# Other partition layout for the q and k tiles, logits as plain float32 products, and 64 transfers for v in an attention and mixture-of-experts kernel

## The chip, the cores and the metric

The kernel runs on one core of a Trainium2 chip. The metric is the time of one execution on the device in microseconds (us); the median of the runs shown is compared. The engines of the core work side by side: PE multiplies matrices (PEld is its loading of weights), DVE, ACT and POOL (GpSimd) work element by element, and SP issues most of the transfers (DMA).

## The reference

What must be computed, cut to what matters here: attention inside chunks of 64 tokens, a routed mixture of 8 experts, and a dense layer with three inputs to a maximum.

```python
B, H, S, D = 8, 8, 576, 64                      # q, k, v: (B, H, S, D), float32
scores = (1 / sqrt(D)) * q_c @ k_c.T            # in each chunk of 64 tokens
attn = softmax(scores); x = attn @ v_c          # x: (B*S = 4608, H*D = 512)
skip = x @ w_skip; compute = skip > 0           # w_skip: (512,)
logits = x[compute] @ w_gate                    # w_gate: (512, 8)
e = argmax(logits); g = softmax(logits)[e]
x[compute] += g * (relu(x[compute] @ w1[e]) @ w2[e])
h = max(x @ m2_w1, x @ m2_w2, x @ m2_w3); out = h @ m2_w_out
```

## The kernel before, in words

The program has three stages. The first, which the change touches, does attention and routing; the second runs the experts on gathered rows; the third is the dense layer.

**Units and steps.** The 4608 tokens are cut into 18 units of 256 tokens (q and k of a unit are loaded together) and 36 tiles of 128 tokens. One loop runs over `t`, 36 tiles and a lag, and everything of a step is written there; a unit `u` is two steps. PE's order is the written order. The order of the other engines comes from a scheduler.

**Loads.** `load_qk(u)` (L212) puts q and k of a unit into tiles of 128 partitions. A partition holds two tokens of all eight heads, so a packet is 512 bytes, and a unit that lies in one batch entry takes one transfer of 128 partitions for q and one for k. A unit across a boundary of batch entries (576 tokens each) takes two for each, with fewer partitions. `load_v(u)` (L221) loads v chunk by chunk of 64 tokens, even heads into partitions 0 to 63 and odd heads into 64 to 127: 64 KB and 64 partitions each, 144 transfers in all. Loads run five units ahead for q and k and three for v. SP takes its transfers in order, and one that must wait for a buffer holds those behind it.

**Turning.** `pair_heads` (L230) copies each half of q and k into an order in which two heads lie side by side: q by POOL, k (`kr`) by DVE. Three buffers each of `qr` and `kr`. `qk_transpose` (L245) turns them on PE, four 128x128 transposes for each of q and k in a step, and ACT copies the result out (L247).

**A step on PE** is, in this order: `values` of tile t-2 (L290, `xp`), `scores` of tile t (L260, `sc`), the transposes of tile t-1's exponentials (L277, `trp`), in every second step the logits (L333, `lt`), the transposes of q and k for unit u+1 (`trq`, `trk`), the transposes of tile t-2's rows (L318, `trx`), and in every other second step the logits' way back (L341, `lp`). DVE makes the maximum and the difference (L264, L266) and the scaled rows (L303 to L305).

**Logits.** The turned rows are split into a rounded part `xh` (ACT, L325) and the remainder `xl` (DVE, L326). Eight products of 18 rows by 256 tokens with the split gate weights `wr` give the logits turned (`lt`), ACT copies them (L335), and two float32 products with a small matrix `fold` bring them back to one token a partition (`lp`). The gates `wcat` are loaded behind unit 4 (L590, L591) and split by ACT and DVE (L592, L593).

**Routing.** For each group of four tiles, `route` does some twenty small DVE operations, `place` two small products (`rk`, L409, L410) and the slots, `store_x` sends 1040 KB of rows to memory on POOL's queue (L470), and `send_id` scatters ids in four indirect transfers by POOL (L448). Weights of expert 0 are loaded and split in the last third of the stage (L91).

Of the kernel before, what the change touches and what calls it, by code (L numbers as in the profile page):

```python
# [37 lines left out]
def kernel(  # L38
# [45 lines left out]
    def ps_sm(name):  # L84
        return ps("sm", name)
# [54 lines left out]
    wr = kpool.tile([P, KC, 2 * R], F32R, name="wr")  # L140
    fold = kpool.tile([P, R], F32, name="fold")
    lgT = kpool.tile([P, UT], F32, name="lgT")
    nc.gpsimd.memset(lgT, 0.0)
    nc.gpsimd.memset(fold, 0.0)
    for base in (0, -R):
        nc.gpsimd.affine_select(
            out=fold, in_=fold, compare_op=ALU.not_equal, fill=1.0, base=base,
            pattern=[[-1, R]], channel_multiplier=1,
        )
# [33 lines left out]
    NV = 4  # L183
    v_all = [apool.tile([P, 4, 4, D + 1], F32, name=f"v_all{i}", bufs=1) for i in range(NV)]
# [16 lines left out]
    def load_qk(u):  # L201
        if u % 5 < 3:
            qt = four_kb([P, H, 2 * D], F32, f"qt{u}", u % 5 == 2)
            kt = four_kb([P, H, 2 * D], F32, f"kt{u}", u % 5 == 2)
        else:
            both = bpool.tile([P, 2, H, 2 * D], F32, tag="b8", name=f"qkt{u}")
            qt, kt = both[:, 0], both[:, 1]
        for h0, h1 in [(0, 4), (4, 8)] if u == 0 else [(0, 8)]:
            for off, b, s, n in pieces(u):
                pr = slice(off // 2, (off + n) // 2)  # L210
                for dst, src in ((qt, q), (kt, k)):
                    link["load"] = nc.sync.dma_start(  # L212
                        dst[pr, h0:h1], src[b, h0:h1, s:s + n, :].rearrange("h (p r) d -> p h (r d)", r=2))
        units[u] = {"qt": qt, "kt": kt}

    def load_v(u):
        vb = v_all[u % NV]
        for off, b, s, n in pieces(u):
            for c in range(n // 64):
                for par in range(2):  # L220
                    link["load"] = nc.sync.dma_start(  # L221
                        vb[64 * par:64 * par + 64, off // 64 + c, :, :D],
                        v[b, par::2, s + 64 * c:s + 64 * c + 64, :].rearrange("hp k d -> k hp d"),
                    )
# [923 lines left out]
```

## Time and profile before

| | |
|---|---|
| median of 3 runs | 1119.62 us (1119.02 to 1122.96) |
| the profiled execution's own time | 1127.18 us |
| its span, first to last instruction | 1125.4 us |
| PE busy | 1024.9 us, 91% of the span |
| DVE, ACT, POOL busy | 596.0, 420.8, 326.1 us |
| mean granted TensorE clock | 0.96 of full |
| moved by DMA | 217.13 MB, mean 193 GB/s |

The attention stage takes about the first 245 us of the span. A busy PE is not a PE at its peak, and the share over the span is a mean over three stages with different limits. So the stage that the change touches is read by itself, by its windows and by what ended PE's idle time in it.

### The profile page before, as it was taken

The page shows a single profiled execution, that of the slowest core. Times are in us where ns is not written, and L with a number is a line of the kernel's source. Part 1 is how long each engine was busy: PE and PEld are TensorE (multiplying, and loading weights), DVE is VectorE, ACT ScalarE, POOL GpSimd, SP SyncE. Part 2 cuts the span into 40 slices and gives each one's busy share as a digit, 9 for nine tenths or more (in the row PEclk, how much of TensorE's full clock was granted, in tenths as well). Part 3 has the DMA queues.
Part 4 walks back from the last instruction along what each step waited for, and adds up shares of the span by engine and source line. Part 5 has one row for each costly group of instructions (what it writes and reads, how often), then busy time and mean ns, then how long its engine had stood idle before and what let it go on. Part 6 is the DMA issues. An engine that isn't in the chain of part 4 may idle for free.

```text
span 1125.4 us, 19554 instructions
## 1 busy us (share of the span) xinstructions
PE 1024.9 (91%) x7472; PEld 863.2 (77%) x7472; DVE 596.0 (53%) x1182; ACT 420.8 (37%) x738; POOL 326.1 (29%) x312
## 2 busy tenths in 40 slices
PE   7687787697899997999899799999999999999997
PEld 5576676585897886888688588878887788888996
DVE  3577677746772845642479881444334352443241
ACT  4455465523542524442344342222322242222231
POOL 2123323247431534450233231111311140122121
PEclk8789889999999998999899999999999999999999
DMA  8889975338671827661998935664456644666591
GB/s 204 168 220 211 241 199 160 128 126 316 219 282 67 279 82 263 204 211 39 292 317 297 318 99 171 184 189 147 163 162 186 195 131 143 194 196 203 175 296 38
DMA packets 214769, 217.13 MB, mean 193 GB/s; under 512 B 49931, under 2 KB 178955, under 8 KB 214656
## 3 DMA queue, kind: packets, MB, share of 16 engines
q1 hardware_dynamic: 201472, 174.18, 53.1%
q0 software_dynamic: 10592, 33.20, 8.3%
q10 hardware_dynamic: 2592, 8.26, 1.8%
q8 instruction: 69, 1.13, 0.4%
q14 instruction: 44, 0.36, 0.1%
HBM read 175.15 MB, written 41.83 MB: 193 GB/s over the span
## 4 chain that ended last, share of the span: by engine, by line
PE 44%; DMA 3%; DVE 1%; issue 1%; POOL 1%; ACT 0%; SPq 0%; POOLq 0%; DVEq 0%; ACTq 0%
PE f_a L705 6%; PE f_a L707 6%; PE f_a L706 6%; PE o L705 4%; PE o L707 4%; PE o L706 4%; PE f_d L705 3%; PE f_d L706 3%; PE f_d L707 3%; DMA ws<-m_sums 2%; PE f_b L705 1%; PE f_b L707 1%; PE f_b L706 1%; PE trf L879 1%; DMA m_sums<-n_q 1%
## 5 line engine op out<-in xcount | busy, mean ns | idle before, releaser
L91 POOL TENSOR_TENSOR fh<-best,fh 128x512 fp32r<-128x512 f32 (+1 forms) x60 | 75.0, 1255 | 354.9 <-ACT fh L90 269.5
L705 PE MATMUL f_a<-x_t,ws 128*128 128x512 f32 (+1 forms) x270 | 100.0, 372 | 2.7 <-ACT u L1044 2.7
L707 PE MATMUL f_a<-x_t,ws 128*128 128x512 f32 (+1 forms) x270 | 99.5, 368 | 0.0
L706 PE MATMUL f_a<-x_t,ws 128*128 128x512 f32 (+1 forms) x270 | 99.4, 368 | 0.0
L705 PE MATMUL h<-xhi,whi_e 128*128 128x256 f32 x256 | 76.4, 299 | 13.9 <-ACTq L982 6.4
L90 ACT CAST whi_e<-raw_e 128x1024 fp32r<-128x1024 f32 x64 | 66.5, 1052 | 60.3 <-DMA raw_e<-in_moe_w_dram 28.2
L706 PE MATMUL o<-wlo_m,fh 128*128 128x512 f32 x216 | 84.6, 391 | 0.0
L705 PE MATMUL o<-whi_m,fh 128*128 128x512 f32 x216 | 83.9, 392 | 0.0
L707 PE MATMUL o<-whi_m,fh 128*128 128x512 f32 x216 | 83.3, 392 | 0.0
L706 PE MATMUL h<-xlo,whi_e 128*128 128x256 f32 x256 | 75.8, 297 | 4.6 <-issue 4.6
L705 PE MATMUL y<-whi_e,hhi 128*128 128x512 f32 x184 | 73.6, 402 | 2.1 <-DMA xg<-x_dram,ids_sb 0.8
L707 PE MATMUL h<-xhi,wlo_e 128*128 128x256 f32 x256 | 74.6, 295 | 0.0
L707 PE MATMUL y<-whi_e,hlo 128*128 128x512 f32 x184 | 71.9, 398 | 2.0 <-DVE hlo L773 1.8
L91 POOL TENSOR_TENSOR wlo_e<-raw_e,whi_e 128x1024 fp32r<-128x1024 f32 x21 | 54.2, 2581 | 65.1 <-ACT whi_e L90 64.6
L706 PE MATMUL y<-wlo_e,hhi 128*128 128x512 f32 x184 | 71.8, 393 | 0.0
L91 DVE TENSOR_TENSOR wlo_e<-raw_e,whi_e 128x1024 fp32r<-128x1024 f32 x43 | 59.1, 1383 | 20.7 <-ACT whi_e L90 10.6
L90 ACT CAST fh<-best 128x512 fp32r<-128x512 f32 (+1 forms) x60 | 34.7, 581 | 90.2 <-DVE best L1035 61.3
L705 PEld LDWEIGHTS h<-xhi,whi_e 128*128 128x128 f32 x256 | 52.5, 205 | 17.0 <-ACTq L982 6.8
L705 PEld LDWEIGHTS f_a<-x_t,ws 128*128 128x128 f32 x270 | 51.0, 189 | 12.0 <-ACT u L1044 3.5
L1038 ACT COPY p<-f_a 128x512 f32<-128x512 f32 (+1 forms) x45 | 24.4, 546 | 91.7 <-PE f_a L707 91.5
L706 PEld LDWEIGHTS f_a<-x_t,ws 128*128 128x128 f32 x270 | 51.0, 189 | 8.4
L707 PEld LDWEIGHTS f_a<-x_t,ws 128*128 128x128 f32 x270 | 50.9, 189 | 8.5
(226 smaller groups left out, 2592.1 us busy)
## 6 DMA issues: line engine op xcount, KB each, us to landing
ws<-m_sums SPq DMA_DIRECT2D x135, 512.0 KB
raw_e<-in_moe_w_dram SPq DMA_DIRECT2D x64, 512.0 KB
ws<-m_sums SPq DMA_DIRECT2D x45, 256.0 KB
v_all<-in_v_dram SPq DMA_DIRECT2D x144, 64.0 KB
x<-x_dram SPq DMA_DIRECT2D x36, 256.0 KB
out_dram<-os SPq DMA_DIRECT2D x36, 256.0 KB
x_dram<-xg POOLq DMA_DIRECT2D x8, 1040.0 KB
m_sums<-n_raw ACTq DMA_DIRECT2D x18, 448.0 KB
```

What stands on the lines that cost most here:

```text
L90: nc.scalar.copy(hi, src),
L91: eng.tensor_tensor(lo, src, hi.bitcast(F32), op=ALU.subtract),
L705: nc.tensor.matmul(acc, ahi, bhi, start=first, stop=False, skip_group_check=onto)
L706: nc.tensor.matmul(acc, ahi, blo, start=False, stop=False, skip_group_check=onto)
L707: return nc.tensor.matmul(acc, alo, bhi, start=False, stop=last, skip_group_check=onto)
L879: nc.tensor.transpose(tr[:, i * P:(i + 1) * P], row[:, c * P:(c + 1) * P], ident)
L1038: nc.scalar.copy(p1, acc_a)
```

## The change

Five things change, all in the first stage.

- **q and k tiles.** A partition now holds four consecutive tokens of four heads: heads 0 to 3 in partitions 0 to 63, heads 4 to 7 in 64 to 127. A packet is 1 KB, and each piece of a unit takes two transfers of at most 64 partitions for q and two for k. The copies and transposes keep their number and size; a transpose now covers one residue of tokens mod 4 for both halves, and the copy out writes with a step of four elements (two before).
- **kr by GpSimd** from unit 2 on.
- **v** by batch entry and head: 64 transfers (the first batch entry's are cut in two, so 72 issues), three buffers of nine chunks.
- **Logits.** ACT copies the turned rows whole (`xt`), and four float32 products a tile (128 tokens by 9) give the logits one token a partition. `xh`, `xl`, `wr`, `fold`, `lt` and the second product are gone. Logits come at lag 3, routing and placing at lags 3 and 4, and the loop is one step shorter.
- **Gates** are loaded behind unit 2 and the rest of the first v. The scratch space of POOL's transfers is halved.

```diff
-            pr = slice(off // 2, (off + n) // 2)
-            for dst, src in ((qt, q), (kt, k)):
-                ... dst[pr, h0:h1], src[b, h0:h1, s:s + n, :].rearrange("h (p r) d -> p h (r d)", r=2)
+            for half in range(2):
+                pr = slice(64 * half + off // 4, 64 * half + (off + n) // 4)
+                for dst, src in ((qt, q), (kt, k)):
+                    ... dst[pr, h0:h1], src[b, 4 * half + h0:4 * half + h1, s:s + n, :].rearrange("h (p r) d -> p h (r d)", r=4)
...
+    def load_v(b, c0=0, c1=CB):
+        for h in range(H):
+            rows = slice(64 * (h % 2), 64 * (h % 2) + 64)
+            link["load"] = nc.sync.dma_start(
+                v_all[b % NV][rows, c0:c1, h // 2, :D],
+                v[b, h, 64 * c0:64 * c1, :].rearrange("(c k) d -> k c d", k=64))
...
-            r = apool.tile([P, 2, H // 2, D], F32, tag=nm + "r", name=f"{nm}r{u}_{g}", bufs=3)
-            (nc.scalar.copy if u == 0 else nc.gpsimd.tensor_copy if nm == "q" and u > 1 else nc.vector.tensor_copy)(
+            r = apool.tile([P, 4, 2, D], F32, tag=nm + "r", name=f"{nm}r{u}_{g}", bufs=3)
+            (nc.scalar.copy if u == 0 else nc.gpsimd.tensor_copy if u > 1 else nc.vector.tensor_copy)(
...
-                dst[:, 2 * g:2 * g + 2, :].rearrange("p h (t r) -> p h r t", r=2), tr)
+                dst.rearrange("p (a j) (t r) -> p j r a t", j=2, r=4)[:, g],
+                tr.rearrange("p r (a t) -> p r a t", a=2))
...
-        nc.scalar.copy(un["xh"][:, :, sl], tr)
-        nc.vector.tensor_tensor(un["xl"][:, :, sl], tr, un["xh"][:, :, sl].bitcast(F32), op=ALU.subtract)
+        xt[t] = apool.tile([P, KC, P], F32, tag="xt", name=f"xt{t}", bufs=2)
+        nc.scalar.copy(xt[t], tr)
+    def logits(t):
+        lp = ps_sm(f"lp{t}")[:, :R]
+        for c in range(KC):
+            link["logits", t] = nc.tensor.matmul(lp, xt[t][:, c, :], wcat[:, c, :], start=c == 0, stop=c == KC - 1)
+        nc.scalar.copy(groups[g][1][:, j, :], lp)
...
-    LAG, late, raws_0 = GT + 6, range(NT - 2), {}
+    LAG, late, raws_0 = GT + 5, range(NT - 2), {}
```

Where the instructions stand shows at three places. First SP's queue in the first units; the number behind `qt`, `kt`, `qkt` is the unit, behind `v_all` the buffer, and the shape is partitions by heads (or chunks) by elements. Before:

```order
L221 DMA v_all1_142<-in_v_dram 64x4x64 x8
L212 DMA qkt3_235<-in_q_dram 128x8x128
L212 DMA qkt3_235<-in_k_dram 128x8x128
L221 DMA v_all2_143<-in_v_dram 64x4x64 x8
L212 DMA qkt4_246<-in_q_dram 64x8x128
L212 DMA qkt4_246<-in_k_dram 64x8x128
L212 DMA qkt4_246<-in_q_dram 64x8x128
L212 DMA qkt4_246<-in_k_dram 64x8x128
L590 DMA wcat_99<-in_moe_w_gate_dram 128x4x8
L591 DMA wcat_99<-in_moe_w_skip_dram 128x4x1
L212 DMA qt5_257<-in_q_dram 128x8x128
L212 DMA kt5_258<-in_k_dram 128x8x128
```

And of the change:

```order
L203 DMA kt2_215<-in_k_dram 48x4x256
L211 DMA v_all0_130<-in_v_dram 64x5x64 x8
L555 DMA wcat_99<-in_moe_w_gate_dram 128x4x8
L556 DMA wcat_99<-in_moe_w_skip_dram 128x4x1
L203 DMA qkt3_234<-in_q_dram 64x4x256
L203 DMA qkt3_234<-in_k_dram 64x4x256
L203 DMA qkt3_234<-in_q_dram 64x4x256
L203 DMA qkt3_234<-in_k_dram 64x4x256
L211 DMA v_all1_131<-in_v_dram 64x9x64 x8
L203 DMA qkt4_247<-in_q_dram 32x4x256
L203 DMA qkt4_247<-in_k_dram 32x4x256
L211 DMA v_all2_132<-in_v_dram 64x9x64 x8
```

The two gate transfers have moved from behind unit 4 to ahead of unit 3, each transfer of unit 3 has become two of 64 partitions, and all of batch entries 1 and 2 of v now stands ahead of units 4 and 5.

Second PE's queue, two steps early in the loop (`sc` of tiles 5 and 6 before, tiles 4 and 5 now). Before, with one line for two products of `lp` and two lines of four for `lt`:

```order
L290 MATMUL xp3_616<-v_all1_142,aT3_577 64x65 x16
L260 MATMUL sc5_645<-kT2_418,qT2_417 64x64 x16
L277 MATMUL trp4_667<-ident_77,ex4_569 128x128 x4
L245 MATMUL trq3_1_674<-ident_77,qr3_1_440 128x128 x4
L245 MATMUL trk3_1_680<-ident_77,kr3_1_442 128x128 x4
L318 MATMUL trx3_686<-ident_77,xg0_381 128x128 x4
L341 MATMUL lp0_693<-fold_101,lgT_102 128x9 x2
L290 MATMUL xp4_704<-v_all2_143,aT4_672 64x65 x16
L260 MATMUL sc6_728<-kT3_590,qT3_589 64x64 x16
L277 MATMUL trp5_750<-ident_77,ex5_664 128x128 x4
L333 MATMUL lt1_757<-xh1_608,wr_100 18x256 x4
L333 MATMUL lt1_757<-xl1_609,wr_100 18x256 x4
```

And of the change:

```order
L247 MATMUL sc4_555<-kT2_425,qT2_424 64x64 x16
L264 MATMUL trp3_577<-ident_77,ex3_489 128x128 x4
L316 MATMUL lp1_584<-wcat_99,xt1_522 128x9 x4
L232 MATMUL trq3_0_592<-ident_77,qr3_0_367 128x128 x4
L232 MATMUL trk3_0_598<-ident_77,kr3_0_369 128x128 x4
L308 MATMUL trx2_604<-ident_77,xg0_388 128x128 x4
L280 MATMUL xp3_615<-v_all0_130,aT3_582 64x65 x16
L247 MATMUL sc5_636<-kT2_425,qT2_424 64x64 x16
L264 MATMUL trp4_658<-ident_77,ex4_574 128x128 x4
L316 MATMUL lp2_665<-wcat_99,xt2_609 128x9 x4
L232 MATMUL trq3_1_671<-ident_77,qr3_1_445 128x128 x4
L232 MATMUL trk3_1_677<-ident_77,kr3_1_447 128x128 x4
```

The eight `lt` products and the two `lp` products of a pair of steps are gone, and each step has four `lp` products between `trp` and `trq`; their inputs are two steps old.

Third POOL's queue around the first stores (L470, now L444) and scatters (L448, now L422). Before:

```order
L230 COPY qr6_0_905<-qt6_354 128x512
L230 COPY qr6_1_1012<-qt6_354 128x512
L470 DMA x_dram_66<-xg0_381 128x4x520
L448 DMA ids_dram_67<-tok_i_120,rslot0_1009 36864x1 x4
L230 COPY qr7_0_1101<-qt7_521 128x512
L301 MEMSET xg2_1122 128x4x7
L230 COPY qr7_1_1194<-qt7_521 128x512
L230 COPY qr8_0_1315<-qkt8_697 128x512
```

And of the change:

```order
L444 DMA x_dram_66<-xg0_388 128x4x520
L219 COPY qr6_0_914<-qt6_357 128x512
L219 COPY kr6_0_916<-kt6_358 128x512
L422 DMA ids_dram_67<-tok_i_109,rslot0_906 36864x1 x4
L219 COPY qr6_1_999<-qt6_357 128x512
L219 COPY kr6_1_1001<-kt6_358 128x512
L291 MEMSET xg2_1108 128x4x7
L219 COPY qr7_0_1087<-qt7_524 128x512
L219 COPY kr7_0_1089<-kt7_525 128x512
L219 COPY qr7_1_1209<-qt7_524 128x512
L219 COPY kr7_1_1211<-kt7_525 128x512
```

Each `qr` copy now has a `kr` copy behind it, so that eight copies instead of four stand in POOL's queue between two groups of four scatters.

## Rows read from the trace of the kernel before

**Rows 1.** Page of the profile: busy time by engine, and DMA share in 40 slices
```profile
PE 1024.9 (91%) x7472; PEld 863.2 (77%) x7472; DVE 596.0 (53%) x1182; ACT 420.8 (37%) x738; POOL 326.1 (29%) x312
...
DMA  8889975338671827661998935664456644666591
```

**Rows 2.** Windows: us, busy PE, PEld, DVE, ACT, POOL, clock, DMA share, GB/s
```profile
0.00:58.00 58.00, 40.01 (x637) 33.18 (x641) 26.14 (x65) 25.96 (x48) 10.57 (x36) 0.79 0.89 190
58.00:155.00 97.00, 79.94 (x1523) 67.71 (x1519) 67.63 (x229) 52.90 (x111) 30.96 (x42) 0.89 0.93 224
155.00:211.00 56.00, 43.59 (x862) 36.35 (x854) 41.85 (x123) 32.36 (x64) 21.17 (x27) 0.94 0.51 151
211.00:245.00 34.00, 26.83 (x259) 23.23 (x251) 21.86 (x102) 11.29 (x24) 9.60 (x11) 0.90 0.32 110
```

**Rows 3.** Timeline of PE, 30 to 59 us: start, length, operation, idle time before
```profile
40.24 1.04 PE L333 MATMUL lt<-xh,wr 128*18 128x256 f32 x4 [7.37 <-DVE wr L593]
...
48.09 0.51 PE L341 MATMUL lp<-fold,lgT 128*128 128x9 f32 x4
48.53 0.70 PE L290 MATMUL xp<-v_all,aT 64*64 64x65 f32 x32
...
50.03 0.71 PE L333 MATMUL lt<-xh,wr 128*18 128x256 f32 x4
...
51.05 0.60 PE L245 MATMUL trq<-ident,qr 128*128 128x128 f32 x4
...
58.16 0.65 PE L260 MATMUL sc<-kT,qT 64*64 64x64 f32 x32
```

**Rows 4.** Waits of PE, 0 to 245 us: total us, times, longest us
```profile
PE sc L260 <- issue: 11.5, 26, 1.1
PE trx L318 <- DVE xg L305: 11.3, 9, 3.4
...
PE rk L410 <- DVE run L378: 5.6, 6, 1.6
PE rk L409 <- DVE roh L374: 2.8, 3, 0.9
...
PE rk L409 <- DVE cnt_i L397: 1.6, 1, 1.6
```

**Rows 5.** Timeline of SP's DMA issues, 20 to 46 us
```profile
22.51 6.66 SPq L221 DMA_DIRECT2D v_all<-in_v_dram  x8
...
32.01 0.62 SPq L590 DMA_DIRECT2D wcat<-in_moe_w_gate_dram  x1
```

**Rows 6.** Windows of single kinds of transfer, columns as in rows 2
```profile
24.00:26.00 2.00, 1.80 (x42) 1.49 (x39) 0.95 (x3) 1.67 (x4) 0.12 (x1) 1.00 1.18 325
27.00:28.00 1.00, 0.00 (x0) 0.00 (x0) 0.24 (x1) 0.09 (x1) 0.05 (x1) 1.00 1.15 183
28.00:30.00 2.00, 0.74 (x4) 0.71 (x4) 1.97 (x5) 0.00 (x0) 0.00 (x0) 0.70 0.44 84
32.00:36.00 4.00, 0.86 (x16) 0.51 (x8) 1.99 (x4) 1.22 (x2) 0.00 (x0) 0.93 1.24 188
112.00:114.00 2.00, 1.36 (x43) 1.04 (x43) 1.16 (x3) 1.23 (x4) 1.70 (x2) 1.00 1.10 336
```

**Rows 7.** DVE groups by line, 58 to 211 us: busy us, mean ns, idle before
```profile
L326 DVE TENSOR_TENSOR xl<-trx,xh 128x512 fp32r<-128x512 f32 x27 | 18.6, 688 | 12.8 <-ACT xh L325 9.8 <-ACT ex L269 2.0 <-issue 0.8
...
L230 DVE COPY kr<-kt 128x512 f32<-128x512 f32 x16 | 6.8, 428 | 5.0 <-PE trk L245 5.0
```

**Rows 8.** POOL groups by line, 58 to 211 us
```profile
L448 POOL DMA_INDIRECT ids_dram<-tok_i,rslot x28 | 28.6, 1022 | 19.1 <-DVE sm L304 7.8 <-issue 6.4 <-DVE rslot L423 5.0
L230 POOL COPY qr<-qt 128x512 f32<-128x512 f32 x15 | 9.3, 619 | 41.1 <-PE trq L245 38.7 <-DMA v_all<-in_v_dram 2.4
L470 POOL DMA_DIRECT2D x_dram<-xg x7 | 5.8, 826 | 19.5 <-PE rk L409 9.5 <-DVE run L378 5.9 <-DVE xg L364 4.1
```

**Rows 9.** Timeline of PE, the last scores
```profile
210.82 0.65 PE L260 MATMUL sc<-kT,qT 64*64 64x64 f32 x32
```

More of the change, by code (lines that the diff above doesn't have):

```diff
@@ L139 @@
     wcat = kpool.tile([P, KC, R], F32, name="wcat")
[L140 to L149, printed above, removed]
     GT = 4
@@ L181 @@
     nc.gpsimd.dma_start(ids_dram.rearrange("(p c) o -> p (c o)", p=P), ids_sb)
-    NV = 4
-    v_all = [apool.tile([P, 4, 4, D + 1], F32, name=f"v_all{i}", bufs=1) for i in range(NV)]
+    NV, CB = 3, S // 64
+    v_all = [apool.tile([P, CB, 4, D + 1], F32, name=f"v_all{i}", bufs=1) for i in range(NV)]
     for i, t in enumerate(v_all):
@@ L281, in exp_transpose, with v_of @@
         un["aT", s] = aT
+    def v_of(chunk):
+        return v_all[chunk // CB % NV][:, chunk % CB]
     def values(t):
@@ L318, in x_transpose @@
             link["x", t] = nc.tensor.transpose(tr[:, c, :], rows_of(t)[:, c * P:(c + 1) * P], ident)
-        u, s = divmod(t, 2)
-        un = units[u]
-        if s == 0:
-            un["xh"] = apool.tile([P, KC, UT], F32R, tag="xh", name=f"xh{u}", bufs=1)
-            un["xl"] = apool.tile([P, KC, UT], F32R, tag="xl", name=f"xl{u}", bufs=1)
-        sl = slice(s * P, s * P + P)
-        nc.scalar.copy(un["xh"][:, :, sl], tr)
-        nc.vector.tensor_tensor(un["xl"][:, :, sl], tr, un["xh"][:, :, sl].bitcast(F32), op=ALU.subtract)
-    def logits(u):
-        un = units[u]
-        lt = ps_sm(f"lt{u}")[:2 * R, :UT]
-        for n, x in enumerate(("xh", "xl")):
-            for c in range(KC):
-                link["logits", u] = nc.tensor.matmul(
-                    lt, wr[:, c, :], un[x][:, c, :], start=n + c == 0, stop=n == 1 and c == KC - 1)
-        nc.scalar.copy(lgT[:2 * R, :], lt)
-    def logits_back(u):
-        g, j = PLACE[2 * u]
-        lp = ps_sm(f"lp{u}")[:, :2 * R].rearrange("p (t r) -> p t r", t=2)
-        for s in range(2):
-            link["back", u] = nc.tensor.matmul(
-                lp[:, s, :], lgT[:, s * P:s * P + P], fold, start=True, stop=True)
-        nc.scalar.copy(groups[g][1][:, j:j + 2, :], lp)
+        xt[t] = apool.tile([P, KC, P], F32, tag="xt", name=f"xt{t}", bufs=2)
+        nc.scalar.copy(xt[t], tr)
+    def logits(t):
+        g, j = PLACE[t]
+        lp = ps_sm(f"lp{t}")[:, :R]
+        for c in range(KC):
+            link["logits", t] = nc.tensor.matmul(lp, xt[t][:, c, :], wcat[:, c, :], start=c == 0, stop=c == KC - 1)
+        nc.scalar.copy(groups[g][1][:, j, :], lp)
     def route(g):
@@ L570, with in_turn, load_gates @@
     AHEAD = 11
-    units, groups, slots, picks, xgs, xT, link, put, sent = {}, {}, {}, {}, {}, {}, {}, {}, []
+    units, xt, groups, slots, picks, xgs, xT, link, put, sent = {}, {}, {}, {}, {}, {}, {}, {}, {}, []
     ids_rows = ids_dram.rearrange("(p c) o -> p (c o)", p=P)
-    def in_turn(load, u):
+    def in_turn(load, *what):
         with tc.issue_after(link["load"].ins) if "load" in link else nullcontext():
-            load(u)
+            load(*what)
+    first_v = {1: [(0, 0, 4)], 2: [(0, 4, CB)], 3: [(1,)], 4: [(2,)]}
+    def load_gates():
+        nc.sync.dma_start(wcat[:, :, :E], w_gate.rearrange("(c p) e -> p c e", p=P))
+        link["load"] = nc.sync.dma_start(wcat[:, :, E], w_skip.rearrange("(c p) -> p c", p=P))
     for u in range(5):
         in_turn(load_qk, u)
-        if 0 < u < 4:
-            in_turn(load_v, u - 1)
+        for part in first_v.get(u, ()):
+            in_turn(load_v, *part)
+        if u == 2:
+            in_turn(load_gates)
         if u < 2:
@@ L623 @@
             exp_transpose(t - 1)
-        if s == 0 and 0 <= u - 2 < NU:
-            logits(u - 2)
+        if 0 <= t - 3 < NT:
+            logits(t - 3)
         if u + 1 < NU:
```

62 lines of the change are left out of this document (23 added, 39 removed).

## The prediction

> **What bounds the kernel now.** I read the page first. PE is busy for 91% of the span, but the share of DMA is high only in the first slices [rows 1]: the first stage has a limit of its own. So I read that stage by windows [rows 2]. In its first 58 us PE is busy for 40.0 us with DMA at 0.89 and a granted clock of 0.79; from 58 to 155 us PE has 79.9 of 97 us; from 155 to 211 us, where expert weights are split as well, PE has 43.6 of 56 us while DVE has 41.9 (75%). No engine is full. PE works in written order, so its idle gaps are what can be won, and the waits of PE name them [rows 4]: 11.3 us for the scaled rows of DVE (`trx`), 5.6 + 2.8 + 1.6 = 10.0 us for the routing on DVE (`rk`), 11.5 us in which `sc` waits for nothing that the profile shows, and one wait of 7.37 us before the first logits, for the split gates [rows 3]. The reader is to see that these are waits for late inputs, mostly DVE's, and one for a late load.
>
> From the scores at 58.16 us (step 8) to the last ones at 210.82 us (step 35) [rows 3, 9] a step takes 152.7 / 27 = 5.65 us.
>
> **The change part by part.** The sum is made against the profiled execution's 1127.18 us; the median of the runs shown is 1119.62 us, so I carry the difference over to it.
>
> *Start.* The gates are issued at 32.01 us behind units 3 and 4, and each unit's v takes 6.66 us of issuing [rows 5]. Now they are ahead of unit 3, and the wait of 7.37 us goes. What is late next are units 4 and 5, behind v entries 1 and 2. Up to unit 5 the queue carries 6 x 1.05 = 6.3 MB of q and k and 3 x 1.18 = 3.5 MB of v. Unit 3, on 128 partitions, ran at 325 GB/s, and unit 4, on 64 at a time, at 188 GB/s with the same 512-byte packets [rows 6]: the new q and k transfers all have at most 64 partitions and are nearest to the second row. A v backlog ran at 183 GB/s [rows 6]. So unit 5 lands at about 6.3 / 0.188 + 3.5 / 0.183 = 52.8 us; some 2 us for the first bytes are balanced by its turning standing some 2.5 us behind the step's start (`xp` at 48.53, `trq` of the next step at 51.05 [rows 3]). With two copies of 0.62 us on POOL [rows 8] step 8 comes at 54 us against 58.16: -4 us. Bounds: at 325 GB/s the loads are no limit and the whole 7.4 us is won; if the halved entry 0 goes at between the 84 GB/s of single 64 KB issues [rows 6] and the backlog's rate, it is +2. The later v transfers carry 147 KB an issue, 2.25 times as much, which at the issue pace of that row would be 189 GB/s, so I take them as no longer held by issuing.
>
> The Trainium skill (page "SBUF — State Buffer", section "Door 1: The DMA port swizzle") says that partitions 0 to 63 reach only half of the ports, and gives 196 GB/s for 64 partitions against 328 for 128. The trace agrees with it (188 against 325). By the page's 196 step 8 would come about 1 us earlier than by the row. It speaks against this change, since every load now has at most 64 partitions.
>
> *Logits on PE.* Two `lp` products take 48.53 - 48.09 = 0.44 us, eight `lt` products 51.05 - 50.03 = 1.02 us [rows 3]. Before, a pair of steps had both, 1.46 us; now it has eight products of the `lp` form, 1.76 us. 18 x 0.30 = +5.4 us. If ACT and DVE delays hide it, it is nothing.
>
> *DVE.* It loses `xl` (0.69 us a tile, behind a wait of up to 9.8 us in total for ACT's rounding) and from unit 2 `kr` (0.43 us) [rows 7], 1.1 us of the some 3.9 us a step that DVE is busy now (67.6 of 97 us at 5.65 a step) [rows 2]. Three things follow. The routing's small operations are reached earlier, and the logits no longer go through `lt`, a copy and `lp` first: of the 10.0 us of `rk` waits [rows 4] I take -7 (0 to -10). Scaled rows come earlier: of 11.3 us I take -3 (0 to -8). Between 155 and 211 us PE idles 56 - 43.6 = 12.4 us [rows 2], part of it counted already, beside a DVE with weight splits; ten steps lose 11 us of DVE work, I take -4 (0 to -8).
>
> *Tail.* Lag and chain: the last placing is one step earlier, and `xl` (0.69) and `lt` (1.02 [rows 3]) leave the last tile's chain: -2 (0 to -4).
>
> *POOL.* 32 more copies of 0.62 us, 20 us. In a group of four steps it then has eight copies, 5.0, four scatters of 1.02, 4.1, and a store issue of 0.83 [rows 8], 9.9 us of 22.6. The cover is the wait for PE: the first `qr` group alone sat idle for 38.7 us until PE gave buffers back [rows 8]. Behind a waiting scatter now stand the next `qr` and `kr`, and behind these PE's transposes. A copy may start once the step before has turned its tiles and is needed two steps later, so I cost it at nothing; without that cover it is 1.24 us a step.
>
> *At nothing:* ACT's whole copy stands for the rounding of the same size; the copies out with a wider step are bounded below by nothing and above by some tenths of a us on ACT, which PE does not wait for. The 11.5 us of `sc` gaps [rows 4] stand where a store of rows moves (336 GB/s in one such window [rows 6]); there are as many stores, so they stay. [...]
>
> Sum: -4 + 5.4 - 7 - 3 - 4 - 2 = -14.6 us, so 1112.6 for the profiled execution and 1105.0 for the median. What a measurement of this kernel can tell from no change is about 0.5%, 5.6 us.
>
> **The rivals.**
> *A, more is won (1091).* The two halves overlap on the wire and DVE's relief removes nearly all waits: -7.4 + 5.4 - 10 - 6 - 7 - 3 = -28. For it: `rk` and `trx` waits are all DVE's. Against it: the 188 GB/s row.
>
> *B, the waits only move (1117).* Start 0, `rk` -4, `trx` -1, the split stretch -2, tail -1, logits +5.4: -2.6. For it: the store gaps and the steps behind them remain, and PE idles there whatever DVE does. That the change does nothing at all is within this case.
>
> *C, loads become the bound (1129, slower).* By step 32, when unit 17 is turned, 18.9 MB of q and k, 8.3 MB of v and seven stores of 1.07 MB must be through. At 188, 183 and 336 GB/s [rows 6] that is 100 + 45 + 22 = 167 us. Step 32 is at 210.82 - 3 x 5.65 = 193.9 us now and about 182 by my sum: 15 us of room. It decides when the loads' mean rate falls under 27.2 MB / 160 us = 170 GB/s. At 150 GB/s they end at 181 + 22 + 2 = 205 us, 11 behind now, less 2 in the tail: +9. For it: DMA has a share of 0.93 between 58 and 155 us [rows 2]. Against it: the share counts queueing packets, and loads ran ahead there.
>
> *D, POOL holds up PE (1129).* If scatters (4.1 us, and idle time of 19.1 / 7 = 2.7 us before a group [rows 8]) hold the copies for longer than the two steps of room, about 11 us now, PE waits; 6.8 + 2 x 1.24 = 9.3 us fits until a step is under 4.7 us. Should it cost 3 us in eight groups: +24 - 14.6.
>
> **How the numbers follow.** Forecast 0.50 (own range 1098 to 1112), A 0.15, B 0.20, C 0.10, D 0.05. Faster by over 0.5% (under 1114.0): nearly all of the forecast, A, and a little of B, 0.69. Within 0.5%: most of B and the edge of the others, 0.18. Slower: C, D and slips, 0.13. The range from 1089 to 1123 leaves out the far end of A and most of C and D, together about 0.2.
>
> **What would show it.** Right: no wait of 7 us before the first logits; step 8 near 54 us; loads of q and k near 190 GB/s in the first 50 us; `rk` waits of some 3 us in all; DVE near 2.8 us a step; the last scores near 199 us; POOL still idle for PE. Wrong: POOL waiting for q and k loads in every step and PE for POOL's copies (C), PE waiting for copies only behind scatters (D), or steps of 5.6 us with gaps in `sc` as long as now (B).

## The result, and the profile after

The changed kernel takes 1134.45 us (median of 4, 1131.08 to 1136.91) against 1120.2 us for the kernel before on the same chip: ratio 1.0131, 95% interval 1.0105 to 1.0157, so 14 us slower. Forecast were 1105.0 us and a range from 1089 to 1123. The profiled execution took 1135.2 us (span 1133.5), 8 us more than the one shown of before, which lay 7 us above its own median. Medians are of all executions of a kernel; the ratios leave out single ones far from the rest, such as one of 2516 us among the ten of run e4 below.

The page after, busy time by engine:

```profile
PE 1030.9 (91%) x7544; PEld 876.2 (77%) x7544; DVE 577.5 (51%) x1113; ACT 445.6 (39%) x737; POOL 337.1 (30%) x339
```

The windows after, columns as in [rows 2]:

```profile
0.00:58.00 58.00, 42.66 (x711) 36.73 (x712) 26.76 (x77) 35.16 (x54) 12.10 (x35) 0.93 1.01 182
58.00:155.00 97.00, 77.63 (x1493) 70.28 (x1492) 54.04 (x169) 60.08 (x100) 47.13 (x69) 0.87 1.12 228
155.00:211.00 56.00, 39.84 (x716) 35.77 (x716) 33.08 (x98) 37.19 (x59) 19.75 (x28) 0.82 0.54 144
```

Between 58 and 155 us DVE is busy for 54.0 us in place of 67.6 (3.1 us a step, 2.8 were forecast), and DMA's share has gone from 0.93 to 1.12. ACT went from 52.9 to 60.1 us, which was not forecast. Between 155 and 211 us PE has 39.8 us, less than the 43.6 of before, where 4 us were to be won.

Three stretches of PE's timeline after (start, length, operation, idle time before); the first two rows are a step's logits and what follows them, the third begins the scores of step 8:

```profile
40.31 0.96 PE L316 MATMUL lp<-wcat,xt 128*128 128x9 f32 x8
41.13 0.63 PE L232 MATMUL trq<-ident,qr 128*128 128x128 f32 x4
...
52.81 0.30 PE L247 MATMUL sc<-kT,qT 64*64 64x64 f32 x8
```

```profile
147.71 0.84 PE L247 MATMUL sc<-kT,qT 64*64 64x64 f32 x26
...
159.41 0.90 PE L264 MATMUL trp<-ident,ex 128*128 128x128 f32 x3 [10.32 <-ACT qT L233]
```

```profile
217.69 0.65 PE L247 MATMUL sc<-kT,qT 64*64 64x64 f32 x32
```

The scores of step 8 start at 52.8 us (before 58.16 [rows 3]). Step 25 starts at 147.7 us; in the trace of before it starts at 154.7, so against that execution 7 us are in hand (a second execution of before, e9, had step 25 at 141.8, and against that one nothing is). Then PE stands idle for 10.32 us, step 26 starts only at 165.8, and the last scores at 217.7 us come 6.9 later than before [rows 9].

From step 25 to step 26 it is 18.1 us, where a step took 5.6 us on average from step 8 on. Besides the idle time there are 3 us of slow work: from 159.4 to 165.8 us the granted clock is 0.53, near the lower of its two levels (1.2 of 2.4 GHz), after 1.00 from 140 to 149 us, and four transposes `trq` last 1.09 us where they lasted 0.63. This one stall of some 13 us, idle time and slow restart together, is more than the lead of 7. PE's waits after, 0 to 245 us:

```profile
PE sc L247 <- ACT kT L233: 16.3, 15, 2.0
PE trp L264 <- ACT qT L233: 12.4, 4, 10.3
...
PE sc L247 <- DVE ex L253: 4.4, 1, 4.4
...
PE sc L247 <- issue: 1.9, 4, 0.7
...
PE rk L383 <- ACT lg L317: 1.7, 1, 1.7
PE trq L232 <- POOL qr L219: 1.6, 2, 1.1
...
PE trx L308 <- DVE xg L295: 0.2, 1, 0.2
```

The waits for routing (`rk`, 10.0 us in [rows 4]) and for scaled rows (`trx`, 11.3 us) are nearly gone. In their place stands ACT: 16.3 us of `sc` for `kT` in 15 portions, and 12.4 us of `trp`, all but 2.1 of it the one stall. Why ACT is late, its groups by line say first (busy us, mean ns, idle before):

```profile
L233 ACT COPY qT<-trq 128x512 f32<-128x512 f32 x36 | 39.2, 1090 | 9.5 <-PE trq L232 9.4
...
L233 ACT COPY kT<-trk 128x512 f32<-128x512 f32 x34 | 37.8, 1111 | 0.5 <-PE trk L232 0.5
```

Before, the copy of `qT` took 633 ns and that of `kT` 624:

```profile
L247 ACT COPY qT<-trq 128x512 f32<-128x512 f32 x36 | 22.7, 633 | 4.9 <-PE trq L245 4.9
```

Then ACT's timeline at the stall, and SP's issue of the weight load after, and before:

```profile
157.33 1.04 ACT L90 CAST whi_e<-raw_e 128x1024 fp32r<-128x1024 f32 x1 [10.67 <-DMA raw_e<-in_moe_w_dram]
158.28 1.08 ACT L233 COPY qT<-trq 128x512 f32<-128x512 f32 x1
```

```profile
148.25 0.61 SPq L97 DMA_DIRECT2D raw_e<-in_moe_w_dram  x1
```

```profile
139.24 0.60 SPq L97 DMA_DIRECT2D raw_e<-in_moe_w_dram  x1
```

ACT takes its instructions in order. The cast of expert 0's first weight tile, `whi_e`, waits 10.67 us for its load, and the copy of `qT` that PE needs stands right behind it (158.28). `trp` waits for a bank of PSUM, the memory in which PE leaves its results, that this copy frees. The load was issued at 148.25 us, behind the q and k of unit 16; before, the same load went out at 139.24.

Two more waits of that kind follow. DVE's timeline at 182 us, and ACT's in expert 0:

```profile
189.37 0.17 DVE L630 TENSOR_SCALAR at<-ids 128x2 int32<-128x2 int32 x1 [6.04 <-DMA ids<-ids_dram]
189.45 0.68 DVE L251 TENSOR_REDUCE mx<-sc 128x8 f32<-128x512 f32 x1
```

```profile
274.17 1.78 ACT L539 CAST n_raw<-n_q 128x896 fp32r<-128x896 f32 x2 [8.01 <-DVE n_q L536]
...
275.85 0.59 ACT L741 ACTIVATE h_0s<-h 128x512 f32<-128x512 f32 x1
```

DVE stands 6.04 us before `at`, which needs the first ids read back from memory, with the next maximum behind it (PE: 4.4 us). And ACT stands 8.01 us before the cast of a sum for the third stage, whose DVE input is not ready, with the ReLU of expert 0's last tile (`h_0s`) behind it; PE waits 7.37 us there. In the kernel before, that ReLU stood ahead of the sum:

```profile
261.97 0.60 ACT L765 ACTIVATE h_0s<-h 128x512 f32<-128x512 f32 x1 [1.67 <-issue]
...
263.91 1.78 ACT L565 CAST n_raw<-n_q 128x896 fp32r<-128x896 f32 x2
```

### The profile page after: what moved, and what is told of

Its sections match the earlier page's. It is cut to its first block, busy times and chain, and to the rows that moved or that the text cites. A ratio compares the mean times of both kernels' runs of the same rounds, so it can differ in the third digit from the quotient of the medians.

```text
span 1133.5 us, 19678 instructions
## 1 busy us (share of the span) xinstructions
PE 1030.9 (91%) x7544; PEld 876.2 (77%) x7544; DVE 577.5 (51%) x1113; ACT 445.6 (39%) x737; POOL 337.1 (30%) x339
## 4 chain that ended last, share of the span: by engine, by line
PE 42%; DVE 3%; DMA 3%; issue 2%; POOL 0%; ACT 0%; SPq 0%; DVEq 0%; ACTq 0%; POOLq 0%
PE f_a L681 5%; PE f_a L683 5%; PE f_a L682 5%; PE o L681 4%; PE o L683 4%; PE o L682 4%; PE f_d L681 3%; PE f_d L683 3%; PE f_d L682 3%; DMA m_sums<-n_q 2%; PE f_b L681 1%; PE f_b L683 1%; PE f_b L682 1%; PE trf L855 1%; DMA ws<-m_sums 1%
## 5 line engine op out<-in xcount | busy, mean ns | idle before, releaser
L91 DVE TENSOR_TENSOR wlo_e<-raw_e,whi_e 128x1024 fp32r<-128x1024 f32 x43 | 53.7, 1263 | 30.1 <-ACT whi_e L90 28.7
```

The lines of the kernel that those rows point to most:

```text
L91: eng.tensor_tensor(lo, src, hi.bitcast(F32), op=ALU.subtract),
```

## The experiments

All times are medians; each ratio is to the kernel before on the same chip. Differences between runs are taken from the ratios, times 1120 us.

| run | what it is | median us | ratio, 95% interval |
|---|---|---|---|
| changed kernel | | 1134.45 | 1.0131, 1.0105 to 1.0157 |
| e7 | before + new q/k layout | 1135.53 | 1.0178, 1.0133 to 1.0223 |
| e4 | changed, q/k layout of before | 1117.05 | 0.9970, 0.9942 to 0.9999 |
| e2 | changed, copies without the step | 1129.81 | 1.0099, 1.0058 to 1.0141 |
| e12 | e4 + sums behind expert 0 | 1110.89 | 0.9920, 0.9897 to 0.9943 |
| e14 | e12 + copies with step of four | 1116.95 | 0.9975, 0.9943 to 1.0007 |
| e13 | e12 + loads of 64 partitions | 1128.45 | 1.0104, 1.0068 to 1.0140 |
| e15 | e12 + split four steps later | 1101.23 | 0.9854, 0.9812 to 0.9896 |
| e1 | changed, split four steps later | 1123.37 | 1.0034, 1.0009 to 1.0060 |
| e3 | changed, weight loads earlier | 1125.24 | 1.0046, 1.0017 to 1.0075 |
| e16 | changed, split and sums later | 1117.14 | 0.9989, 0.9960 to 1.0018 |
| e17 | e16, split two steps later still | 1121.84 | 1.0019, 0.9990 to 1.0049 |
| e5 | e3 + ids one step later | 1121.87 | 1.0029, 1.0000 to 1.0058 |
| e6 | e4 + both moves of e5 | 1114.52 | 0.9977, 0.9952 to 1.0001 |
| e8 | before + early gates | 1118.88 | 0.9998, 0.9971 to 1.0024 |
| e10 | e8 + weight loads earlier | 1119.53 | 0.9996, 0.9974 to 1.0017 |
| e11 | e4, kr on VectorE | 1120.95 | 0.9992, 0.9958 to 1.0027 |
| e9 | before again | 1118.39 | 0.9998, 0.9974 to 1.0022 |

e2 and e14 leave the tokens of a unit in another order, so their attention is over other groups of tokens and other rows go to the experts. They are set beside the others up to the last scores; behind these their times are those of another problem.

### The layout of q and k: e7 and e4

e7 does this part alone on the kernel before; e4 undoes it alone in the changed kernel (the same lines the other way):

```diff
-  qt, kt: [P, H, 2 * D]; one transfer of up to 128 partitions; copy out "p h (t r)" with r=2
+  qt, kt: [P, H // 2, 4 * D]; two transfers of up to 64 partitions; copy out "(t r)" with r=4
```

> The kernel before with the new q and k tiles alone (four tokens of four heads, 1 KB packets into 64 partitions, copies with a step of four); logits, gates, v and kr as before. Theory C, the layout itself costs: copies of some 1090 ns in place of 630, PE waits for kT by some 10 us in all, and the kernel takes 4 to 14 us more than before (1124 to 1134). Rival: the layout only costs where the other parts let PE run ahead, since before the change PE waits for other things at the same points; then the time stays within 3 us of before.

> The changed kernel with the q and k tiles as before (two tokens of eight heads in a partition, 512 byte packets over 128 partitions, copies out with a step of two); all other parts stay changed. Theory B plus C: the 64-partition transfers and the step of four are what cost; copies fall to some 630 ns, the waits for q, kT and the weights go, and the kernel takes 14 to 24 us less than the changed kernel (1110 to 1120), that is, as much as before or less. Theory A alone: with loads issued as before the wait for the weights goes too, but the wait for kT remains; 8 to 12 us less. Rival: what cost lies in the other parts (kr on GpSimd, v transfers), and the time stays within 4 us of the changed kernel.

e7 is 1.8% slower than before, more than expected, and e4 is 18 us faster than the changed kernel. So the layout alone accounts for the loss, on either base; the other parts together are worth 3 us as they stand, not the 14.6 of the sum. In e7 the stall at step 25 is there too (PE idle 16.0 us). The rival that the layout costs only where PE runs ahead falls.

### Copies or loads: e2, e14, e13

e2 takes the step out of the changed kernel's copies:

```diff
-  dst.rearrange("p (a j) (t r) -> p j r a t", j=2, r=4)[:, g]
+  dst.rearrange("p (a j) (r t) -> p j r a t", j=2, r=4)[:, g]
```

> The changed kernel with the copies out of the transposes of q and k written to contiguous columns, so that the tokens of a unit stand in another order: the attention is over other groups of tokens and the routing that follows differs, so only the part up to the last scores is compared. Theory C, the step of four elements in the copy's output is what made it 1090 ns where it was 634: each copy takes 600 to 650 ns, ScalarE is busy some 32 us less, PE's wait of 16.3 us for kT falls below 5, and the last scores start 8 to 14 us earlier than at 217.7. Rival: the copies' length is hidden (ScalarE waits for PE anyway) and the last scores move by less than 4 us.

One row of ACT's groups, and PE's timeline at the stall:

```profile
L233 ACT COPY qT<-trq 128x512 f32<-128x512 f32 x36 | 20.7, 575 | 11.5 <-PE trq L232 11.4
```

```profile
139.97 0.65 PE L247 MATMUL sc<-kT,qT 64*64 64x64 f32 x32
158.24 1.12 PE L264 MATMUL trp<-ident,ex 128*128 128x128 f32 x4 [17.62 <-ACT qT L233]
```

The copies fell to 575 and 585 ns and the wait for `kT` from 16.3 to 4.9 us, and step 25 started 7.7 us earlier, at 140.0 (in part this may be the execution's: e1, e16 and e17, which are the changed kernel up to step 22, start step 25 at 142.3, 142.8 and 149.6). But the weight tile landed when it had before (PE resumes at 158.24, in the changed kernel at 159.41), so the stall grew to 17.62 us, and the last scores came only 3.1 us earlier. The number is the rival's, the mechanism is neither's: the copies do hold PE up, and the stall behind them takes it back.

e14 and e13 do one half of the layout each, on e12, which has the tiles of before (and the sums moved, below):

```diff
 e14:
-  dst[:, 2 * g:2 * g + 2, :].rearrange("p h (t r) -> p h r t", r=2), tr
+  dst.rearrange("p (a j) (t r) -> p j r a t", j=2, r=4)[:, g], tr.rearrange("p h r (a t) -> p (h r) a t", a=2)
 e13:
-  pr = slice(off // 2, (off + n) // 2)
+  for i in range(0, n, 128):  # 64 partitions at a time, 512 byte packets
+      pr = slice((off + i) // 2, (off + i + m) // 2)
```

> The same kernel (1110.89) with its loads of 128 partitions, but the copies out of the transposes of q and k written with a step of four; the tokens of a unit then stand in another order, so the attention is over other groups and the routing differs from the reference's. If the copies carry most of the layout's loss: copies of some 1090 ns, PE waits for kT by 10 us or more, last scores 8 to 14 us later than 197.2, 7 to 14 us slower. Rival, they are hidden behind PE: last scores within 4 us of 197.2 and the time within 4 us of 1111.

> The kernel with the q and k tiles of before, all other parts of the change and the sums behind expert 0's last tile (1110.89), with each load of q and k cut into two of 64 partitions, 512 byte packets as before; copies as before. If the narrow transfers alone bring the weights and the units late: 6 to 14 us slower (1117 to 1125), with ScalarE waiting for the first weight tile about as long as in the changed kernel. Rival, the copies with a step of four are the whole loss of the layout: within 3 us of 1111.

ACT's groups of e14:

```profile
L233 ACT COPY qT<-trq 128x512 f32<-128x512 f32 x36 | 39.4, 1100 | 7.5 <-PE trq L231 7.5
```

Copies of 1100 and 1123 ns put the last scores off by 3.8 us (201.0 against 197.2). So of the 460 ns more of each of 70 copies, 32 us of ACT, about an eighth comes through to PE, although its waits for `kT` went from 0.2 to 13.4 us; up to the last scores the rival holds. The whole time is 6 us longer, between the two expectations, but what of this lies behind the last scores cannot be put down to the copies. The narrow loads cost 18 to 21 us by themselves (17.6 by medians, 20.6 by ratios; last scores at 216.2), more than expected, with copies as short as before (617 and 623 ns). When the first weight load is issued and its cast runs, in e12, then in e13, then (the cast) in e14:

```profile
136.51 1.46 SPq L97 DMA_DIRECT2D raw_e<-in_moe_w_dram  x1
```

```profile
144.11 1.04 ACT L90 CAST whi_e<-raw_e 128x1024 fp32r<-128x1024 f32 x1 [3.29 <-DMA raw_e<-in_moe_w_dram]
```

```profile
150.09 0.62 SPq L97 DMA_DIRECT2D raw_e<-in_moe_w_dram  x1
```

```profile
158.49 1.04 ACT L90 CAST whi_e<-raw_e 128x1024 fp32r<-128x1024 f32 x1 [16.52 <-DMA raw_e<-in_moe_w_dram]
```

```profile
144.23 1.04 ACT L90 CAST whi_e<-raw_e 128x1024 fp32r<-128x1024 f32 x1 [5.22 <-DMA raw_e<-in_moe_w_dram]
```

With wide loads the load goes out at 136.5 us and the cast runs at 144.1, whatever the copies take; with narrow ones it goes out at 150.1 and runs at 158.5, as in the changed kernel (148.25 and 157.33). The windows of e12, then of e13, show the rate behind it:

```profile
0.00:58.00 58.00, 44.05 (x798) 38.04 (x799) 26.96 (x82) 30.25 (x58) 14.76 (x39) 0.91 1.02 197
58.00:155.00 97.00, 79.11 (x1515) 71.79 (x1514) 57.53 (x176) 50.34 (x108) 46.56 (x68) 0.88 1.12 244
```

```profile
0.00:58.00 58.00, 42.06 (x709) 36.20 (x709) 25.56 (x77) 27.81 (x54) 11.48 (x34) 0.94 1.03 177
58.00:155.00 97.00, 72.41 (x1493) 65.78 (x1493) 54.69 (x169) 47.35 (x101) 47.53 (x70) 0.90 1.17 226
```

Up to its weight load, e12 had moved 0.197 x 58 + 0.244 x 78.5 = 30.6 MB by these means, e13 0.177 x 58 + 0.226 x 92.1 = 31.1 MB: about the same bytes, 13.6 us later, at a DMA share over 1 in both. By this share transfers stand queued nearly all the time, so what is queued last comes later by the whole difference. 512-byte packets (e13) and 1 KB packets (the changed kernel) end in the same place, so it is not the size of the packets. Cutting the loads also doubles their number, and no run parts that from the fewer partitions; but e13 has the higher share (1.17 against 1.12) at the lower rate, so its packets take longer, which a higher number of issues does not explain by itself.

### The waits in order: e1, e3, e16, e17

```diff
 e1:  if t % 2 == 0 and 0 <= t - 22 <= 16:  ->  0 <= t - 26 <= 16      # loads and splits of expert 0
 e3:  load_raw two units ahead of its split, splits where they stand
 e16: e1, and the sums of the third stage recorded behind single("0_2", ...)
 e17: e16 with t - 28
```

> The changed kernel with the loads and splits of expert 0's weights four steps later (from step 26 on in place of 22). Theory A, ScalarE blocked in order: the 18 us between the scores of steps 25 and 26 are ScalarE standing 10.7 us before the cast of a weight tile that has not landed, with the copies out of PSUM queued behind it; then that wait goes, steps 25 to 26 take 4 to 6 us, and the kernel takes 8 to 12 us less than the changed kernel (1122 to 1126). Theory B, the q and k loads are late themselves at that point: the stall only moves to the wait of GpSimd for the q tile, and the time falls by less than 3 us (1131 or more).

> The changed kernel with each weight load of expert 0 issued two units (four steps) earlier than its split, the splits where they stand. Theory A: the weights have landed when ScalarE comes to the cast, the 10.7 us wait is gone, 8 to 12 us less than the changed kernel. Theory B: the weight loads take their share of the same backlog from the q and k loads ahead of step 26, and the wait turns up as GpSimd waiting for q; less than 3 us gained.

e1 and e3 gain 11 and 9.5 us: ACT's wait in order is worth what theory A said. But not all of it goes; in e1 PE's timeline has, at step 29:

```profile
171.22 1.12 PE L264 MATMUL trp<-ident,ex 128*128 128x128 f32 x4 [5.91 <-ACT qT L233]
```

since the load is now queued behind a whole batch entry of v.

> The changed kernel with both moves (splits four steps later, sums behind expert 0's last tile), its q and k layout kept. If the two blocked stretches of ScalarE add up: 11 and 6 us less than the changed kernel's 1134.45, 1115 to 1120, and what is left against 1110.89 is the copies. Rival: they share one cause in the loads and do not add: 1121 or more.

16 us are gained, as much as e1's 11 and e12's 6 (below) together, so the two waits of ACT add up, with the layout kept. What is left against e15 is 15 us. In e16 ACT still stands before the first cast:

```profile
169.71 1.04 ACT L90 CAST whi_e<-raw_e 128x1024 fp32r<-128x1024 f32 x1 [9.12 <-DMA raw_e<-in_moe_w_dram]
```

> The changed kernel with the sums behind expert 0's last tile and the weight loads and splits of expert 0 six steps later than in the changed kernel (two later than in the run that took 1117.14, where ScalarE still stood 9.1 us before the first cast and PE 9.5 us behind it). If the narrow loads cost only through that wait in order: no such wait, some 7 to 10 us less (1107 to 1110), so that what is left against the wide loads' 1101.23 is the copies (6 us by the run with the copies alone). Rival: the loads bound the stage, so the wait turns up at q, k or v, or the last splits come late for expert 0: 1114 or more.

Here my theory falls. The wait before the cast is gone, but 1121.84 us is not faster (ratio 1.0019, e16 0.9989). DVE waits for the ids in its place:

```profile
176.35 0.17 DVE L630 TENSOR_SCALAR at<-ids 128x2 int32<-128x2 int32 x1 [6.46 <-DMA ids<-ids_dram]
```

PE stands 5.0 us behind it, and expert 0's last splits end up at 218 to 220 us with ACT waiting 3.5 us for a weight load. So with the narrow loads there are further waits behind that one; how much of e16's 15 us each is worth is not shown.

### The ids: e5 and e6

```diff
-  if 0 <= t - 4 < NT:   # place, store_x, scatters, ids read back
+  back = t - (5 if t < 34 else 4)
```

> The changed kernel with expert 0's weight loads two units earlier and, besides, the ranks, scatters, row stores and the reading back of the first ids one step later, where they stood before the change (five steps behind the last tile of a group in place of four). Theory D, VectorE blocked in order by the ids: with the weights early alone, the scores of steps 29 to 30 stood 14.6 us apart, with VectorE 10.2 us idle until the ids had been read back; one step later the wait shrinks by a step or more, and the kernel takes 4 to 9 us less than that one's 1125.2 (1116 to 1121). Rival: the scatters move with the wait, so the ids land a step later too, the wait stays as it was, and the time is 1124 or more.

> Both of these moves on the kernel that has the q and k tiles of before and all other parts of the change (1117.05). If the three causes stand apart (copies with a step of four, ScalarE behind the weights, VectorE behind the ids) this has none of them: its 13.3 us between the scores of steps 25 and 26 become 5, and it takes 1106 to 1111, 0.8 to 1.3% less than before, close to the sum of the prediction. Rival: the attention stage is bound by the loads of q, k and v, so the time waited for weights turns up as waits for q and k, and it takes 1114 or more.

e5 gains 2 to 3 us on e3, within both intervals, less than theory D's 4 to 9; the wait for the ids fell from 10.2 to 3.5 us in the trace, but PE then runs at a granted clock of 0.77 from 155 to 211 us, in many short waits. e6 misses: 1114.52, the rival's number, with no stall at step 25 (4.1 us from there to step 26), but steps of 5.2 to 10.3 us from 26 to 32, at a granted clock of 0.80 from 155 to 211 us where e4 had 0.94. The waits that the rival expects, for q and k, are not in PE's waits there. The clock in this window goes with the execution too: the two profiles of the kernel before have 0.94 and 0.81. Neither run settles what the ids cost by themselves.

### The other parts: e8, e10, e11, e9

```diff
 e8 (on before):   gate loads moved behind the v of unit 1, before unit 3
 e10:              e8, and load_raw two units ahead of its split
 e11 (on e4):      kr by VectorE again
```

> The kernel before with only the loads of the gate weights moved ahead, behind the v of the second unit, the logits still as split products. The prediction's first term: the wait of 7.4 us of the first logits goes, step 8 starts some 4 us earlier than at 58.2, and 2 to 5 us of that are left at the end (1115 to 1118). Rival: a lead of a few us at step 8 is eaten by a later wait for a load, and the time stays within 2 us of before.

Step 8 starts at 54.9 and step 25 at 138.8, 3.2 and 15.9 us earlier than in the profile that the prediction read, but only 1.3 and 3.0 earlier than in the second one of before (e9: 56.2 and 141.8). At the end nothing of the lead is left: ratio 0.9998. ACT's timeline of e8:

```profile
146.83 1.04 ACT L90 CAST whi_e<-raw_e 128x1024 fp32r<-128x1024 f32 x1 [8.97 <-DMA raw_e<-in_moe_w_dram]
```

> The kernel before with the gate weights early and, besides, each weight load of expert 0 issued two units earlier. The gates alone moved nothing (1118.88, ratio 0.9998), and in their profile PE stood idle 8.5 us behind the weights at step 25. Theory E: with the weights early too, that wait goes and 4 to 8 us of the lead are kept (1111 to 1115). Rival: the loads of q, k and v then come later by as much and a later wait eats the lead: 1117 or more.

That wait went, and the time did not move. SP's issues and DVE's wait in e10:

```profile
178.09 1.28 SPq L221 DMA_DIRECT2D v_all<-in_v_dram  x2
179.69 0.35 SPq L464 DMA_DIRECT2D ids<-ids_dram  x1
```

```profile
182.84 0.17 DVE L655 TENSOR_SCALAR at<-ids 128x2 int32<-128x2 int32 x1 [12.79 <-DMA ids<-ids_dram]
```

The reading back of the ids stood in SP's queue behind small transfers of v and weight loads until 179.69 us, though the last scatter ahead of it had been issued by 169.3, and DVE waited 12.79 us for it (PE 11.6). The rival's time holds, and a later wait does eat the lead, but it is one for the ids and not for q, k or v.

> The kernel with the q and k tiles of before and all other parts of the change (1117.05), with the copies into kr back on VectorE from unit 2 on (428 ns each in the profile of before, GpSimd's 620). If relief of VectorE was worth something by itself (the prediction's terms for the waits of ranks and rows): 3 to 8 us slower than 1117. Rival: what is gained ahead of step 26 waits there for the weights, and what GpSimd takes over shows up as its own wait (kr 3.6 us): within 3 us of 1117, either way.

e11 and e4 differ by 2.5 us, within the intervals: not told apart from nothing.

> The kernel before, unchanged, for a second profile: the one shown took 1127.18, some 7 us above the median of its executions. Theory E, the time up to the scores of step 26 is set by when expert 0's first weight tile lands, not by the work ahead: in an execution near the median the scores of step 25 start some 5 to 15 us earlier than at 154.7, and a wait of ScalarE for the weights with PE idle behind it stands there (steps 25 to 26 over 8 us). Rival: the faster executions are faster all along or in the expert stage, step 25 starts at 150 or later, and no wait for the weights is there.

The second profile of before took 1113.79 us. Rows of its timeline and of its waits:

```profile
141.80 0.65 PE L260 MATMUL sc<-kT,qT 64*64 64x64 f32 x32
...
149.88 1.08 PE L260 MATMUL sc<-kT,qT 64*64 64x64 f32 x32
```

```profile
PE sc L260 <- issue: 3.6, 3, 1.8
```

Step 25 starts at 141.8, 13 us earlier than in the profile that the prediction read, and the gaps of `sc` are 3.6 us, not 11.5 [rows 4]. Steps 25 to 26 take 8.1 us, as theory E says, but ACT's wait for the weights is 2.3 us and PE's idle time behind it 1.6: half of that expectation holds. So the room that I read from one execution was partly that execution's. And against this one the changed kernel is not ahead at step 25 but 5.9 us behind (147.7), and its last scores (217.7) come 14 us later than these at 203.5.

### Sums behind expert 0: e12, and the version that beats both: e15

```diff
-  with tc.issue_after(link["rows"][0].ins), ...:
-      for chunk in later: chunk()
   single("0_2", (0, 2), *third, turn_next)
+  with tc.issue_after(link["hs"].ins), ...:      # hs: the last tile's ReLU
+      for chunk in later: chunk()
```

> The kernel with the q and k tiles of before and all other parts of the change (1117.05), with the two sums of the third stage that are made during expert 0 recorded behind its last tile in place of ahead of it. Theory F, ScalarE blocked in order again: in the changed kernel and its kin ScalarE stands some 8 to 11 us before the cast of a sum whose VectorE operand is not ready, with the ReLU of expert 0's last tile queued behind it, and PE waits 6.9 to 8.7 us; in the kernel before the ReLU stood ahead. With the sums behind it the wait goes and 4 to 7 us are gained (1110 to 1113). Rival: the sums are then late for the third stage, or a wait for expert 1's weights takes the place, and the time stays within 2 us of 1117.

ACT's timeline of e12 in expert 0:

```profile
249.76 0.60 ACT L740 ACTIVATE h_0s<-h 128x512 f32<-128x512 f32 x1 [2.12 <-PE h L682]
...
256.92 1.78 ACT L538 CAST n_raw<-n_q 128x896 fp32r<-128x896 f32 x2 [2.29 <-DVE n_q L535]
```

The ReLU now stands ahead of the sum's cast, PE's wait (6.9 us in e4) is gone, and e12 is 5.6 us faster than e4. The order decides in every profile: from expert 0's first product to the turning of `h_0s` (`trh`) it is 6.7 to 6.8 us in the six runs with the sums behind, 14.2 to 15.7 in the eight with the change's logits and the sums ahead, and 6.4 to 6.5 in the five on the kernel before. Nothing of the change asks for the other order: the scheduler set it, and ACT's order of the two could have been read before the run.

> The same kernel (1110.89) with expert 0's weight loads and splits four steps later. Its profile still has an 11.0 us step at the first split (25 to 26) and one of 10.0 us at the second. If the split's wait for the landing still sets these: 2 to 6 us faster (1105 to 1109). Rival: expert 0's weights are then late for its first products, or the wait only moves: within 2 us of 1111 or slower.

e15 gains 7 to 10 us more, beyond what was expected, and is 1.5% faster than before; its last scores start at 185.6 us.

## Why the prediction was wrong

The step that failed is the price of the q and k layout. The prediction had its two costs before it, and its sum has both at nothing.

- **Copies out.** They were bounded "above by some tenths of a us on ACT, which PE does not wait for". Each took 460 ns more, 32 us of ACT in all, and PE waits 16.3 us for `kT`. By themselves they put the last scores off by 3.8 us (e14). The nearest row was the copy with a step of two at 630 ns; nothing in that trace showed a step of four, so the bound above should have been open. The Trainium skill (page "SBUF — State Buffer", section "Door 1: The DMA port swizzle") says that SBUF has lines of 16 bytes, that each access which crosses to a new line pays, and that four float32 are as far as one may stride for free. The prediction did not weigh that sentence; in this case a step of two took 630 ns against 575 with none, and a step of four, 16 bytes, is not free but takes 1090.
- **Loads.** The rate was right: 188 GB/s was forecast, and in a window of q and k alone after the change it is

```profile
54.00:58.00 4.00, 2.38 (x38) 2.22 (x39) 1.91 (x3) 2.21 (x5) 0.62 (x1) 0.78 1.15 198
```

198. What failed is rival C's test. It asked whether q, k and v reach PE in time by step 32, found 15 us of room and set the turning point at 170 GB/s. They do reach PE in time. What does not is the load queued behind them, expert 0's first weight tile, which ACT's cast waits for ahead of the copies that PE needs. With narrow loads it is issued 13.6 us later and its cast runs 14.4 us later, and the kernel is 18 to 21 us slower (e13). The Trainium skill (page "SBUF — State Buffer", section "Can I just issue two DMAs to hit both halves?") says that only one transfer across all 128 partitions reaches all ports; e13, which differs from e12 in that alone, agrees (226 against 244 GB/s from 58 to 155 us).

The two halves together are more than the layout's 15 to 20 us (e16, e4, e7): with the narrow loads, longer copies matter less (3.1 us at the last scores, e2), since PE waits at the cast anyway.

The other steps, in the order of the sum:

- **Start, -4.** Right in place: step 8 at 52.8, forecast 54. Over the second profile of before (56.2) that is a lead of 3.4 us, over the first 5.4. Alone it is worth nothing (e8): a lead is only kept if nothing later waits for a fixed moment.
- **Logits, +5.4.** A step's eight `lp` rows take 41.13 - 40.31 = 0.82 us, 1.64 a pair against 1.76; so 18 x 0.18 = +3.2.
- **DVE's relief, -10.** The waits fell by more than forecast (`rk` 10.0 to 2.0 us, `trx` for scaled rows 11.3 to 0.2), but in the changed kernel nothing of it shows in the time: waits for ACT took their place. What `kr` alone gives cannot be told from nothing (e11).
- **Split stretch, -4.** Wrong in sign. I priced DVE's relief there and not ACT's wait for the weights, which a faster PE meets sooner: e4 has it with the layout of before (PE idle 6.3 us), and e15, with the split later, gains 7 to 10 us.
- **Tail, -2.** Not won: from the last scores to the first transposes of gathered rows it is 12.0 us (217.7 to 229.7), before 11.3 (210.8 to 222.1). From 223.6 to 229.7 us the granted clock is 0.50, its lower level.
- **POOL, nothing.** Right for the changed kernel: PE waits 1.6 us for `qr`, 0.7 for `kr`, and rival D falls. With ACT's waits mostly gone (e12) it is 2.9 and 4.8 us, so part of this was hidden behind ACT.
- **Gaps of `sc`.** They were to stay at 11.5 us. They are 1.9 after, but 3.6 in the second profile of before, so most of them were that execution's.
- **Not in the sum:** ACT's order of the sum and the ReLU, 5.6 us (e12).

From e15 back to the changed kernel the ratios give 7.4 us for the split (e12), 5.6 for the sums (e4) and 18.0 for the layout; on e15's own base the layout costs 15 (e16). -16.4 + 7.4 + 5.6 + 18.0 comes to the measured loss, as it must, since these are the steps of one chain. That e15's gain of 16 us is near the forecast 14.6 may be luck: e15 has two moves that the forecast did not have, and the later split was not tried on the kernel before. It stays open how the narrow loads cost what they cost once the split is out of the way (e16, e17), and what the ids cost by themselves. The third stage, from its first to its last product, is 4 us longer in the profile after than in the one shown of before (573.6 and 569.4 us); other profiles have 569.7 (e8) to 576.7 (e5), so it may be a difference between executions, and no run was made on it.

## What to carry to other kernels

When a change makes one engine faster, look on every in-order queue for the first instruction that waits for something with its own clock (a weight load, ids coming back, a side job), and for what PE needs behind it: that instruction sets the end, and a lead up to it is worth nothing. When loads run at their limit, ask not only whether what PE uses next is there, but when the last thing in their queue lands. A bound on a copy holds only for the step it was measured with.

## What the runs showed that I had not expected

- A 128x512 float32 copy from PSUM by ACT took 575 ns with no step in its output, 630 with a step of two elements and 1090 with a step of four (e2 and the changed kernel differ in the output's step alone).
- Cutting the q and k transfers into two of half the partitions, at equal bytes and packets, put off a load queued behind 31 MB by 13.6 us.
- Two executions of one kernel, 1113.8 and 1127.2 us, differ by 13 us at step 25 already; a trace's stalls are partly its own, and a second profile of the same kernel helps to tell which.
- In e6 no idle stretch of PE between 155 and 211 us is longer than 2.2 us, and its granted clock there is 0.80 all the same (e4: 0.94). What makes the difference is open.
